# Batch 0's v through casting DMAs, batch 1's loads behind a gate, and a redealt first chain in an attention-and-mixer kernel

## The chip, the cores and the metric

The kernel runs on one core of a Trainium2 chip. The metric is device time in microseconds (us), the median of a few runs. Its engines are TensorE (PE, with its weight loads as PEld), VectorE (DVE), ScalarE (ACT), GpSimd (POOL) and SyncE (SP). DMAs are issued here by SP and by POOL, each into a queue of its own, and run on 16 DMA engines that the core's queues share.

## The reference

Eight batches, eight heads, 576 positions, head size 64. Linear attention gives x for each batch, and a mixer with a low-rank mix over positions and a two-layer product follows:

```
r_q, r_k = relu(q), relu(k)                       # (S, 64) per head
q_p, k_p = [r_q * cos, r_q * sin], [r_k * cos, r_k * sin]      # (S, 128)
kv  = k_p^T v                                     # (128, 64)
z   = sum over S of k_p                           # (128)
x   = (q_p kv) / (q_p z + 1e-6)                   # heads side by side: (576, 512)

u   = x + ((x^T U) V)^T                           # U: 576 x 32, V: 32 x 576
out = u + relu(u w1) w2                           # w1: 512 x 2048, w2: 2048 x 512
```

## The kernel before

The 576 positions of a batch lie in five chunks: four of 128 rows, and a tail (chunk 4) of 64. One partition holds four or five neighbouring positions, so a load of q, k or v is an odd and an even part (`load_odd`, `load_even`, L71 to L81) into the float tiles `qst`, `kst`, `vst`, which all batches share. SP issues them in program order. POOL issues the loads of U and V and of the weights, the latter casting from float to bf16 on the way (`w1_load`, `w2_load`, four loads of 512 KB written each).

The order of work is written out by hand: every engine runs its instructions in program order and waits by semaphores. The stretch that matters here has these steps.

1. Start: memsets, constants, loads of q, k and v of batch 0 on SP, U and V on POOL. POOL's casts of V and U (`cast_uv`). PE runs products of zeros (`keep_warm`, L198).
2. Features of q: `q_prep` (cos and sin weights times relu, L287 on ACT, L289 on DVE), then transposes on PE (`qtr_mm`, L368) and copies to `q_pT` by `qtr_evac`.
3. Features of k, and z by `z_mm` (L883) chunk by chunk, with fillers by `keep_warm` between.
4. `first_chain`: batch 0 from kv to uT. `kv_unit` (L323) makes kv for four heads; `den_mm` (L892) the denominators for four heads; `recip` (L403, L404); `xh_mm` (L903) and `xh_norm` (L912) x for one chunk and four heads; `a_mm` (L439) the product x^T U, called A; `open_mm` (L926) transposes x into a PSUM bank of uT, and `uTd_mm` (L531) adds V's part to it; `uTd_evac` copies uT out. The denominators and z_sb's source lie in the bank pair `xz` (tag X), as does A.
5. The first product with w1 for batch 0, `g1_main` (L551): 16 blocks j of four products each, ACT's relu to `hid` (L560) after each. The first three j begin with half their products, for the first two of four uT parts. Beside the j's run batch 1's steps: `q_prep(1, c)`, `qtr_unit(1, c)` (L356), `k_prep(1, c)`, `v_prep(1, ...)` and batch 0's `u_va` and `u_add` (L464, L473); the table `beside` says after which j each is put.
6. The product with w2 for batch 0 (`g2_part`, L611), with batch 1's kv and x beside it, and so on through the batches.

POOL issues w1's first load between its two casts of batch 0's v tail. Its next steps are the other w1 loads, then a small copy `mark` (L1017) that reads the first half of batch 1's `vst` and so waits for it, then the four w2 loads. SP loads batch 1's q, k and v as soon as the tiles are free, and at slot 15 comes a `gate` (L1033): a tiny DMA that reads a given tile, so that SP stands until this is written, with the loads of batch 2 behind it.

Of the kernel before, what the change touches and what calls it, by code (L numbers as in the profile page):

```python
# [17 lines left out]
def kernel(  # L18
# [91 lines left out]
    def cast(eng, o, i):  # L110
        if eng is nc.scalar:
            nc.scalar.activation(out=o, in_=i, func=AF.Copy, bias=0.0, scale=1.0)
        else:
            eng.tensor_copy(out=o, in_=i)  # L114
# [12 lines left out]
    load_even(qst, q, 0)  # L127
    load_odd(kst, k, 0)
    load_even(kst, k, 0)
    for h0 in (0, 4):  # L130
        load_odd(vst, v, 0, h0, h0 + 4)
        load_even(vst, v, 0, h0, h0 + 4)
    def load_uv():
        nc.gpsimd.dma_start(out=stV, in_=moe_V)
        nines_u = moe_U.rearrange("(m k) r -> m (k r)", k=9)
# [80 lines left out]
    def cast_uv():  # L216
        nine_v = stV.rearrange("r (m k) -> r k m", k=9)
        for i in range(2):
            cast(
                G_,  # L220
                V_nat[:, 0:512].rearrange("r (c m i) -> r c m i", c=4, i=2)[:, :, :, i],
                nine_v[:, 5 * i : 5 * i + 4, :],
            )
        cast(G_, V_nat[:, 512:S], nine_v[:, 4, :])
        cast(G_, U_bf[:, 0:4, :], stU[:, 0:4, :])
        for i in range(2):
            cast(G_, U_bf[tail(i), 4 + i, :], stU[tail(i), 4, :])
# [87 lines left out]
    def kv_unit(b, hg, tag, bufs, eng=None):  # L315
        if b not in kv_sb:
            kv_sb[b] = pool.tile([P, H, E], BF16, tag="kv", bufs=2, name="kv")
        acc = bank([P, 4, E], FP32, tag, bufs, "kv_ps")
        vx = v_ext[b % 2]
        for i in range(4):  # L320
            h = hg * 4 + i
            for c in range(5):
                nc.tensor.matmul(  # L323
                    out=acc[:, i, :],
                    lhsT=k_p[b][:, c, h, :] if c < 4 else k_tl[:, h, :],
                    rhs=v_tl[:, h, :] if c == 4 and b < 2 else vx[:, c, h, :],
                    start=(c == 0),
                    stop=(c == 4),
                )
        cast(eng or V_, kv_sb[b][:, hg * 4 : hg * 4 + 4, :], acc)  # L330

    def kv_pair(b, tag, bufs):
        kv_sb[b] = pool.tile([P, H, E], BF16, tag="kv", bufs=2, name="kv")
# [575 lines left out]
    def xh_norm(b, c, h0, rec, acc):  # L909
        x_alloc(b)  # L910
        rows = slice(0, P) if c < 4 else tail(b)
        nc.vector.tensor_tensor(  # L912
            out=x_of(b, c, rows)[:, h0 * D : h0 * D + 4 * D].rearrange(
                "p (i d) -> p i d", d=D
            ),
            in0=acc[rows],
            in1=rec[rows, c, :].unsqueeze(2).to_broadcast([P if c < 4 else TS, 4, D]),
            op=ALU.mult,
        )

# [3 lines left out]
    def open_mm(b, d, t, cs):  # L924
        for c in cs:
# [2 lines left out]
                start=(c == 0), stop=False,  # L928
            )

    def first_chain(b, xz, v_ps):
        z = xz[:, 0, 0:H]
        d = [
            xz[:, 0, H + 20 * i : H + 20 * i + 20].rearrange("p (c h) -> p c h", h=4)
            for i in range(2)
        ]
        rec = [pool.tile([P, 5, 4], FP32, tag="rec5", bufs=2, name="rec5") for _ in d]
        for h0 in (0, 4):
            v_block(b, h0, h0 + 4, 0, 4, V_)
        cast(V_, V_bf, v_ps.rearrange("r (c p) -> r c p", c=4))  # L940
        cast(A_, z_sb, z)
        kv_unit(b, 0, *T1, A_)
        den_mm(b, 0, 4, d[0])
        recip(rec[0], d[0])
        x0 = [xh_mm(b, c, 0, *t) for c, t in zip(ORD, (G3, G3, G3, OA, OB))]
        den_mm(b, 4, 8, d[1])
        kv_unit(b, 1, *T1, A_)
        for n in range(2):
            xh_norm(b, ORD[n], 0, rec[0], x0[n])
        recip(rec[1], d[1])  # L950
        for n in range(2, 5):
            xh_norm(b, ORD[n], 0, rec[0], x0[n])
        x1 = [xh_mm(b, c, 4, *t) for c, t in zip(ORD[0:4], (G3, G3, G3, OA))]
        for n in range(2):
            xh_norm(b, ORD[n], 4, rec[1], x1[n])
        uT_alloc(b)
        a_ps = xz[:, 1, 0:P]
        a_mm(b, a_ps, (0, 1), range(5))
        cast(A_, A_of(b)[0:TS, :], a_ps[0:TS, :])
        x1.append(xh_mm(b, ORD[4], 4, *G3))  # L960
        for n in range(2, 5):
            xh_norm(b, ORD[n], 4, rec[1], x1[n])
        for i, (tag, bufs) in enumerate((T1, OB, OA)):
            uT_ps[b, i] = bank([P, 4, P], FP32, tag, bufs, "uT_ps")
        for i in range(2):
            open_mm(b, i, uT_ps[b, i], range(4))
        uTd_mm(b, 0)
        uTd_evac(b, 0, A_)
        uTd_mm(b, 1)
        uTd_evac(b, 1, V_)  # L970
        a_mm(b, a_ps, (2, 3), range(5))
        cast(A_, A_of(b)[TS:P, :], a_ps[TS:P, :])
        open_mm(b, 2, uT_ps[b, 2], range(4))
        u3 = ps.tile([P, 2, 512], FP32, tag="X", bufs=1, name="u3")
        uT_ps[b, 3] = u3[:, 0, :].rearrange("p (c t) -> p c t", c=4)
        open_mm(b, 3, uT_ps[b, 3], range(4))
# [40 lines left out]
    G_.tensor_copy(out=mark, in_=vst[0:TS, 3, 4, 0:1])  # L1017
    for n in range(4):
        w2_load(n)
    g1_main(0, 0, True)  # L1020
    uTd_close(0, 2, V_)
    uTd_close(0, 3, A_)
    g1_main(0, 1, True)
    g1_main(0, 2, True)
    q_prep(1, 4, (V_, A_))
    q_prep(1, 0, (V_, V_))


    def at(j, *thunks):
        beside.setdefault(j, []).extend(thunks)  # L1030

    def gate(src):
        nc.sync.dma_start(out=mark2, in_=src)  # L1033
# [12 lines left out]
    for hg in range(2):  # L1046
        at(16 + hg, lambda hg=hg: kv_unit(1, hg, "T", 1))

# [75 lines left out]
```

## Time and profile before

| | |
|---|---|
| median of 3 runs | 301.11 us (299.45 to 301.7) |
| profiled execution, its own time | 301.89 us |
| its span, first to last instruction | 300.1 us |
| mean granted TensorE clock | 0.998 |
| PE busy | 288.3 us (96%) |
| DVE, ACT, POOL busy | 186.3 (62%), 157.4 (52%), 72.7 (24%) |
| DMA | 53.31 MB, mean 178 GB/s |
| chain that ended last | PE 88%, DMA 6%, DVE 2% |
| first product with w1 (L551) | at 23.17 us |
| first product with w2 (L611) | at 40.53 us |

A profile line names the engine, the line of the kernel, the operation, what is written from what, and the count. In a row of the timeline the first two numbers are the start and the length in us; in brackets stands the idle time of the engine before it and what ended it. Matmuls overlap, so a row's length for PE is not the sum of its instructions.

### The profile page before, as it was taken

The page shows a single profiled execution, that of the slowest core. Times are in us where ns is not written, and L with a number is a line of the kernel's source. Part 1 is how long each engine was busy: PE and PEld are TensorE (multiplying, and loading weights), DVE is VectorE, ACT ScalarE, POOL GpSimd, SP SyncE. Part 2 cuts the span into 40 slices and gives each one's busy share as a digit, 9 for nine tenths or more (in the row PEclk, how much of TensorE's full clock was granted, in tenths as well). Part 3 has the DMA queues.
Part 4 walks back from the last instruction along what each step waited for, and adds up shares of the span by engine and source line. Part 5 has one row for each costly group of instructions (what it writes and reads, how often), then busy time and mean ns, then how long its engine had stood idle before and what let it go on. Part 6 is the DMA issues. An engine that isn't in the chain of part 4 may idle for free.

```text
span 300.1 us, 7027 instructions
## 1 busy us (share of the span) xinstructions
PE 288.3 (96%) x2917; PEld 194.5 (65%) x2948; DVE 186.3 (62%) x360; ACT 157.4 (52%) x268; POOL 72.7 (24%) x113
## 2 busy tenths in 40 slices
PE   8999999999989979999999999999999999999993
PEld 6675455545977536865787546865787547845982
DVE  4988748886894657647736577648744685504251
ACT  2935561586672446936584356846693453067300
POOL 8430500050271500550032500550051100400130
PEclk9999999999999999999999999999999999999999
DMA  6999999999979999999659906997366104030004
GB/s 204 351 271 256 219 188 254 284 235 241 278 201 201 131 254 230 210 268 298 177 105 230 336 3 151 223 283 207 72 111 184 39 2 87 2 140 2 0 26 153
DMA packets 85282, 53.31 MB, mean 178 GB/s; under 512 B 54018, under 2 KB 82978, under 8 KB 85250
## 3 DMA queue, kind: packets, MB, share of 16 engines
q1 hardware_dynamic: 78802, 41.40, 59.3%
q0 software_dynamic: 6368, 11.43, 16.2%
q8 instruction: 23, 0.38, 0.5%
q14 instruction: 9, 0.07, 0.1%
q10 hardware_dynamic: 80, 0.03, 0.0%
HBM read 36.86 MB, written 9.44 MB: 154 GB/s over the span
## 4 chain that ended last, share of the span: by engine, by line
PE 88%; DMA 6%; DVE 2%; issue 1%; SPq 1%; ACT 1%; ACTq 0%
PE g_ps L551 35%; PE w_ps L720 27%; PE gt_ps L571 5%; PE o_ps L611 5%; DMA q_pT<-q_p 4%; PE ot_ps L638 3%; PE x_ps L413 3%; DMA qst<-in_q_dram 2%; PE kv_ps L339 2%; PE w_ps L198 1%; PE va_ps L464 1%; PE a_ps L439 1%; PE kv_ps L323 1%; PE t_ps L368 1%; PE t_ps L356 1%
## 5 line engine op out<-in xcount | busy, mean ns | idle before, releaser
L560 ACT ACTIVATE hid<-g_ps 128x512 bf16<-128x512 f32 x128 | 76.1, 597 | 87.2 <-PE g_ps L551 59.9
L551 PE MATMUL g_ps<-uT,w_bf 128*128 128x512 bf16 x491 | 119.4, 379 | 1.3 <-DMA w_bf<-in_moe_w_ch_dram 0.3
L551 PEld LDWEIGHTS <-w_bf 128*128 128x128 bf16 x512 | 46.3, 98 | 49.2 <-issue 0.2
L732 POOL TENSOR_TENSOR o_sb<-w_sum,u_bf 128x512 f32<-128x512 f32 x21 | 26.3, 1278 | 120.7 <-DVE w_sum L732 120.7
L720 PEld LDWEIGHTS <-hid 128*128 128x128 bf16 x448 | 43.7, 98 | 5.6
L720 PEld LDWEIGHTS <-S 128*128 128x128 bf16 x336 | 32.5, 98 | 5.2 <-DVE S L697 1.2
L732 DVE TENSOR_TENSOR o_sb<-o_sb,w_ps 128x512 f32<-128x512 f32 x28 | 19.3, 688 | 18.0 <-PE w_ps L720 11.7
L720 PE MATMUL w_ps<-T,S 128*128 128x256 bf16 x224 | 26.1, 273 | 0.9 <-DVE S L697 0.9
L720 PE MATMUL w_ps<-w_bf,hid 128*128 128x256 bf16 x224 | 26.7, 273 | 0.0
L720 PE MATMUL w_ps<-T,hid 128*128 128x256 bf16 x224 | 26.7, 273 | 0.0
L473 DVE TENSOR_TENSOR u_bf<-x_bf,va_ps 128x1024 bf16<-128x1024 bf16 x16 | 19.3, 1218 | 6.7 <-PE va_ps L464 6.7
L114 POOL CAST v_ext<-vst 128x512 bf16<-128x512 f32 (+1 forms) x30 | 18.6, 658 | 16.8 <-DMA vst<-in_v_dram 13.7
L423 DVE TENSOR_TENSOR x_bf<-x_ps,rec 128x512 bf16<-128x512 f32 x28 | 19.4, 692 | 1.0
L697 DVE TENSOR_TENSOR S<-hid 128x1024 bf16<-128x1024 bf16 x14 | 9.6, 688 | 16.5 <-ACT hid L560 16.5
L403 DVE TENSOR_SCALAR rec<-x_ps 128x8 f32<-128x8 f32 (+1 forms) x35 | 5.8, 164 | 21.7 <-PE x_ps L413 21.6
L287 ACT ACTIVATE k_p<-kst,sinw 128x512 bf16<-128x512 f32 x29 | 18.9, 710 | 0.0
L585 POOL DMA_DIRECT2D out_dram<-o_sb x12 | 7.6, 633 | 44.8 <-DVE o_sb L732 23.2
L413 PEld LDWEIGHTS <-q_pT 128*128 128x128 bf16 x224 | 10.8, 98 | 7.9 <-DMA q_pT<-q_p 2.2
L114 DVE CAST kv<-kv_ps 128x520 bf16<-128x520 f32 (+1 forms) x8 | 5.1, 632 | 17.2 <-PE kv_ps L339 13.7
L287 ACT ACTIVATE q_p<-qst,cosw 128x512 bf16<-128x512 f32 x23 | 15.5, 711 | 0.1
L611 PE MATMUL o_ps<-w_bf,hid 128*128 128x512 bf16 x61 | 15.3, 379 | 0.2
L571 PE MATMUL gt_ps<-uT_tl,w_bf 128*128 128x128 bf16 x256 | 15.1, 219 | 0.0
(145 smaller groups left out, 367.7 us busy)
## 6 DMA issues: line engine op xcount, KB each, us to landing
qst<-in_q_dram SPq DMA_DIRECT2D x14, 512.0 KB, 6.8
kst<-in_k_dram SPq DMA_DIRECT2D x14, 512.0 KB, 8.9
vst<-in_v_dram SPq DMA_DIRECT2D x12, 512.0 KB, 6.8
out_dram<-o_sb POOLq DMA_DIRECT2D x12, 512.0 KB, 6.1
w_bf<-in_moe_w_ch_dram POOLq DMA_DIRECT2D x8, 512.0 KB, 11.1
out_dram<-o_sb SPq DMA_DIRECT2D x4, 512.0 KB, 3.0
qst<-in_q_dram SPq DMA_DIRECT2D x2, 640.0 KB, 7.1
kst<-in_k_dram SPq DMA_DIRECT2D x2, 640.0 KB, 11.0
```

Of the source, the lines that this page charges most:

```text
L114: eng.tensor_copy(out=o, in_=i)
L287: nc.scalar.activation(out=o, in_=i, func=AF.Relu, bias=0.0, scale=w)
L413: nc.tensor.matmul(out=acc[:, g, i * E : i * E + E], lhsT=qT_of(b, c, h), rhs=kv_sb[b][:, h, :], start=True, stop=True,)
L423: nc.vector.tensor_tensor(out=x_of(b, c, rows).rearrange("p (g i d) -> p g i d", g=2, d=D), in0=view[:, :, :, 0:D], in1=rec[rows].unsqueez ...
L473: nc.vector.tensor_tensor(out=u_bf[b][:, d0 : d0 + 2], in0=x_bf[b].rearrange("p c (d n) -> p d c n", n=P)[:, d0 : d0 + 2], in1=va_ps[b, d0 ...
L551: nc.tensor.matmul(out=g_ps.rearrange("p (c t) -> p c t", c=4), lhsT=w1_bf[:, d, j * P : j * P + P], rhs=uT[b][:, d, :, :], start=(d == 0) ...
L560: nc.scalar.activation(out=hid[b][:, j, :], in_=g_ps, func=AF.Relu, bias=0.0, scale=1.0)
L571: nc.tensor.matmul(out=g_ps[:, jj, :], lhsT=w1_bf[:, d, j * P : j * P + P], rhs=uT_tl[pr][:, d, :], start=(d == 0), stop=(d == 3),)
L611: nc.tensor.matmul(out=o, lhsT=hid[0][:, j, cc * P : cc * P + P], rhs=w2_bf[:, j, :], start=(j == 0), stop=(j == NJ - 1),)
L697: V_.tensor_tensor(out=o, in0=a, in1=b_, op=op)
L720: nc.tensor.matmul(out=res[:, g, :], lhsT=lhs[:, k_, g * P : g * P + P], rhs=rhs[:, k_, :], start=(opens and k_ == 0 and g == 0), stop=(k_ ...
L732: eng.tensor_tensor(out=o, in0=x, in1=y, op=ALU.add)
```

## The change

Batch 0's v no longer comes through `vst` and casts. A tile `v0` (it takes the place of the later `hid`) is filled by four casting DMAs that POOL issues, behind its casts of V. The casts of U (`cast_u`) are split off and come after w1's first load. `kv_unit` for batch 0 reads `v0` and makes 64 columns for each head, not 65. `first_chain` makes the denominators of all eight heads at once, with one `recip`, and deals its copies out anew: V's spread copy, both of the first two uT copies and the first x of chunk 3 go to ACT, the second half of A goes to a bank of its own and to DVE, and the last copy of `q_pT` to DVE. Five of the nine fillers beside k's features go. SP has a `gate` on batch 0's kv in front of batch 1's loads. The last two uT products are put ahead of the first w1 products. Batch 1's q features are all given to DVE, after j 2 to 6 (they were ahead of j 0 and after j 0 to 2), its transposes after j 5 to 9 (were 1 to 5), and `spread_tail` after j 12 (was 7).

```diff
@@ start
-    for h0 in (0, 4):
-        load_odd(vst, v, 0, h0, h0 + 4)
-        load_even(vst, v, 0, h0, h0 + 4)
+    v0 = pool.tile([P, H, 5, D], BF16, tag="hid", bufs=1, name="v0")
+    V_.memset(v0[:, :, 4, :], 0.0)
+
+    def v0_load(h0, h1):
+        nc.gpsimd.dma_start(
+            out=v0[1:P:2, h0:h1, 0:4].rearrange("m h c d -> m h (c d)"),
+            in_=nines(v, 0)[:, h0:h1, 5 * D : 9 * D],
+        )
+        nc.gpsimd.dma_start(
+            out=v0[0:P:2, h0:h1].rearrange("m h c d -> m h (c d)"),
+            in_=nines(v, 0)[:, h0:h1, 0 : 5 * D],
+        )
+
@@ kv_unit
-        acc = bank([P, 4, E], FP32, tag, bufs, "kv_ps")
+        n = D if b == 0 else E
+        acc = bank([P, 4, n], FP32, tag, bufs, "kv_ps")
...
-                    rhs=v_tl[:, h, :] if c == 4 and b < 2 else vx[:, c, h, :],
+                    rhs=(
+                        v0[:, h, c, :] if b == 0
+                        else v_tl[:, h, :] if c == 4 and b < 2 else vx[:, c, h, :]
+                    ),
...
-        cast(eng or V_, kv_sb[b][:, hg * 4 : hg * 4 + 4, :], acc)
+        cast(eng or V_, kv_sb[b][:, hg * 4 : hg * 4 + 4, 0:n], acc)
@@ new
+    def xh_norm_act(b, c, h0, rec, acc):
+        x_alloc(b)
+        rows = slice(0, P) if c < 4 else tail(b)
+        for i in range(4):
+            nc.scalar.activation(
+                out=x_of(b, c, rows)[:, (h0 + i) * D : (h0 + i) * D + D],
+                in_=acc[rows, i, :], func=AF.Copy, bias=0.0,
+                scale=rec[rows, c, h0 + i : h0 + i + 1],
+            )
+
@@ first_chain
-        for h0 in (0, 4):
-            v_block(b, h0, h0 + 4, 0, 4, V_)
-        cast(V_, V_bf, v_ps.rearrange("r (c p) -> r c p", c=4))
-        cast(A_, z_sb, z)
+        d = xz[:, 0, H : H + 40].rearrange("p (c h) -> p c h", h=H)
+        rec = pool.tile([P, 5, H], FP32, tag="rec5", bufs=1, name="rec5")
+        cast(A_, z_sb, xz[:, 0, 0:H])
         kv_unit(b, 0, *T1, A_)
-        den_mm(b, 0, 4, d[0])
-        recip(rec[0], d[0])
+        cast(A_, V_bf, v_ps.rearrange("r (c p) -> r c p", c=4))
+        den_mm(b, 0, H, d)
+        recip(rec, d)
         x0 = [xh_mm(b, c, 0, *t) for c, t in zip(ORD, (G3, G3, G3, OA, OB))]
-        den_mm(b, 4, 8, d[1])
         kv_unit(b, 1, *T1, A_)
-        for n in range(2):
-            xh_norm(b, ORD[n], 0, rec[0], x0[n])
-        recip(rec[1], d[1])
-        for n in range(2, 5):
-            xh_norm(b, ORD[n], 0, rec[0], x0[n])
+        xh_norm_act(b, ORD[4], 0, rec, x0[4])
+        for n in range(4):
+            xh_norm(b, ORD[n], 0, rec, x0[n])
...
-        uTd_mm(b, 0)
-        uTd_evac(b, 0, A_)
-        uTd_mm(b, 1)
-        uTd_evac(b, 1, V_)
-        a_mm(b, a_ps, (2, 3), range(5))
-        cast(A_, A_of(b)[TS:P, :], a_ps[TS:P, :])
+        for i in range(2):
+            uTd_mm(b, i)
+            uTd_evac(b, i, A_)
+        a2 = bank([P, P], FP32, *G3, "a_ps")
+        a_mm(b, a2, (2, 3), range(5))
+        cast(V_, A_of(b)[TS:P, :], a2[TS:P, :])
@@ k's features
-    keep_warm(2, *T1)
     for c in TL:
         k_prep(0, c, (V_, A_))
-        keep_warm(2 if c < 2 else 1, *T1)
+        if c < 3:
+            keep_warm((1, 2, 1)[c], *T1)
+        if c == 3:
+            v_ps = spread_v(*OB)
         z_mm(0, c, xz[:, 0, 0:H])
         if c == 1:
             qtr_evac(0, 4, V_, t_q[4])
-    v_ps = spread_v(*OB)
-    qtr_evac(0, 3, A_, t_q[3])
-
-    v_prep(0, 0, 4, (4,), (G_,))
+    qtr_evac(0, 3, V_, t_q[3])
...
+    for h0 in (0, 4):
+        v0_load(h0, h0 + 4)
     w1_load(0)
-    v_prep(0, 4, 8, (4,), (G_,))
+    cast_u()
     for n in range(1, 4):
         w1_load(n)
     first_chain(0, xz, v_ps)
+    gate(kv_sb[0][0:1, 0, 0:1])
     load_odd(qst, q, 1)
...
-    g1_main(0, 0, True)
     uTd_close(0, 2, V_)
     uTd_close(0, 3, A_)
-    g1_main(0, 1, True)
-    g1_main(0, 2, True)
-    q_prep(1, 4, (V_, A_))
-    q_prep(1, 0, (V_, V_))
+    for j in range(3):
+        g1_main(0, j, True)
...
     for n, c in enumerate(ORD):
-        if n > 1:
-            at(n - 2, lambda c=c: q_prep(1, c, (V_, V_)))
+        at(2 + n, lambda c=c: q_prep(1, c, (V_, V_)))
         tg = T1 if n % 2 else O2()
-        at(1 + n, lambda c=c, tg=tg: qtr_unit(1, c, eng=V_, tag=tg[0], bufs=tg[1]))
+        at(5 + n, lambda c=c, tg=tg: qtr_unit(1, c, eng=V_, tag=tg[0], bufs=tg[1]))
...
-    at(7, lambda: spread_tail(*O2()))
+    at(12, lambda: spread_tail(*O2()))
```

More of the change, by code (lines that the diff above doesn't have):

```diff
@@ L224, in cast_uv, with cast_u @@
         cast(G_, V_nat[:, 512:S], nine_v[:, 4, :])
+    def cast_u():
         cast(G_, U_bf[:, 0:4, :], stU[:, 0:4, :])
@@ L916, in xh_norm @@
             in0=acc[rows],
-            in1=rec[rows, c, :].unsqueeze(2).to_broadcast([P if c < 4 else TS, 4, D]),
+            in1=rec[rows, c, h0 : h0 + 4].unsqueeze(2).to_broadcast([P if c < 4 else TS, 4, D]),
             op=ALU.mult,
@@ L929, in open_mm @@
             )
-    def first_chain(b, xz, v_ps):
[L932 to L937, printed above, removed]
-        for h0 in (0, 4):
-            v_block(b, h0, h0 + 4, 0, 4, V_)
-        cast(V_, V_bf, v_ps.rearrange("r (c p) -> r c p", c=4))
-        cast(A_, z_sb, z)
+    def xh_norm_act(b, c, h0, rec, acc):
[7 more added lines that the diff above has]
+            )
+    def first_chain(b, xz, v_ps):
+        d = xz[:, 0, H : H + 40].rearrange("p (c h) -> p c h", h=H)
+        rec = pool.tile([P, 5, H], FP32, tag="rec5", bufs=1, name="rec5")
+        cast(A_, z_sb, xz[:, 0, 0:H])
         kv_unit(b, 0, *T1, A_)
-        den_mm(b, 0, 4, d[0])
-        recip(rec[0], d[0])
+        cast(A_, V_bf, v_ps.rearrange("r (c p) -> r c p", c=4))
+        den_mm(b, 0, H, d)
+        recip(rec, d)
         x0 = [xh_mm(b, c, 0, *t) for c, t in zip(ORD, (G3, G3, G3, OA, OB))]
-        den_mm(b, 4, 8, d[1])
         kv_unit(b, 1, *T1, A_)
-        for n in range(2):
-            xh_norm(b, ORD[n], 0, rec[0], x0[n])
-        recip(rec[1], d[1])
-        for n in range(2, 5):
-            xh_norm(b, ORD[n], 0, rec[0], x0[n])
+        xh_norm_act(b, ORD[4], 0, rec, x0[4])
+        for n in range(4):
+            xh_norm(b, ORD[n], 0, rec, x0[n])
         x1 = [xh_mm(b, c, 4, *t) for c, t in zip(ORD[0:4], (G3, G3, G3, OA))]
         for n in range(2):
-            xh_norm(b, ORD[n], 4, rec[1], x1[n])
+            xh_norm(b, ORD[n], 4, rec, x1[n])
         uT_alloc(b)
@@ L961, in first_chain @@
         for n in range(2, 5):
-            xh_norm(b, ORD[n], 4, rec[1], x1[n])
+            xh_norm(b, ORD[n], 4, rec, x1[n])
         for i, (tag, bufs) in enumerate((T1, OB, OA)):
@@ L993 @@
     xz = ps.tile([P, 2, 512], FP32, tag="X", bufs=1, name="xz")
-    keep_warm(2, *T1)
+    v_ps = None
     for c in TL:
         k_prep(0, c, (V_, A_))
-        keep_warm(2 if c < 2 else 1, *T1)
+        if c < 3:
+            keep_warm((1, 2, 1)[c], *T1)
+        if c == 3:
+            v_ps = spread_v(*OB)
         z_mm(0, c, xz[:, 0, 0:H])
@@ L1000, with gate @@
             qtr_evac(0, 4, V_, t_q[4])
-    v_ps = spread_v(*OB)
-    qtr_evac(0, 3, A_, t_q[3])
-    v_prep(0, 0, 4, (4,), (G_,))
+    qtr_evac(0, 3, V_, t_q[3])
+    def gate(src):
+        nc.sync.dma_start(out=mark2, in_=src)
+    for h0 in (0, 4):
+        v0_load(h0, h0 + 4)
     w1_load(0)
-    v_prep(0, 4, 8, (4,), (G_,))
+    cast_u()
     for n in range(1, 4):
@@ L1019 @@
         w2_load(n)
-    g1_main(0, 0, True)
     uTd_close(0, 2, V_)
     uTd_close(0, 3, A_)
-    g1_main(0, 1, True)
-    g1_main(0, 2, True)
-    q_prep(1, 4, (V_, A_))
-    q_prep(1, 0, (V_, V_))
+    for j in range(3):
+        g1_main(0, j, True)
     def at(j, *thunks):
         beside.setdefault(j, []).extend(thunks)
-    def gate(src):
-        nc.sync.dma_start(out=mark2, in_=src)
     for n, c in enumerate(ORD):
-        if n > 1:
-            at(n - 2, lambda c=c: q_prep(1, c, (V_, V_)))
+        at(2 + n, lambda c=c: q_prep(1, c, (V_, V_)))
         tg = T1 if n % 2 else O2()
-        at(1 + n, lambda c=c, tg=tg: qtr_unit(1, c, eng=V_, tag=tg[0], bufs=tg[1]))
+        at(5 + n, lambda c=c, tg=tg: qtr_unit(1, c, eng=V_, tag=tg[0], bufs=tg[1]))
         at(9 + n, lambda c=c: k_prep(1, c, (V_, A_)))
```

## The prediction

> **What bounds the kernel now.** I read PE's waits first, then the busy time by stretch, then the first 41 us of the timeline, then the DMA queues in that stretch. All times are of the profiled execution, in us from the start of its span. Who made PE wait:
>
> ```profile
> PE x_ps L413 <- DMA q_pT<-q_p: 1.7, 1, 1.7
> PE w_ps L720 <- DVE S L697: 0.9, 1, 0.9
> ...
> PE xh_ps L903 <- ACT kv L112: 0.5, 1, 0.5
> PE u L926 <- ACT A_sb L112: 0.3, 1, 0.3
> PE g_ps L551 <- DMA w_bf<-in_moe_w_ch_dram: 0.3, 1, 0.3
> ```
>
> Once the first product with w1 (L551) has begun, PE waits only twice for longer than 0.3, at 82 (0.9) and at 105.6 (1.7). Busy time by stretch (length, PE, PEld, DVE, ACT, POOL, clock, DMA share, GB/s):
>
> ```profile
> 15.60:23.10 7.50, 6.56 (x160) 5.39 (x161) 5.91 (x17) 2.09 (x6) 2.24 (x3) 1.00 1.16 263
> 23.10:40.50 17.40, 17.23 (x120) 8.70 (x122) 13.76 (x27) 11.54 (x22) 4.45 (x9) 1.00 1.10 223
> 40.50:79.00 38.50, 38.22 (x394) 22.05 (x398) 28.43 (x58) 20.06 (x36) 5.40 (x8) 1.00 1.13 250
> ```
>
> From 23.1 to 79 PE is full, and its work there is not changed. So the change is worth what it moves at 40.5, where PE leaves the first w1 stage for w2 (L611): earlier or later there is earlier or later at the end. The rows of the timeline that I use:
>
> ```profile
> 15.28 0.34 PE L883 MATMUL xz<-v_tl,k_tl 128*128 128x1 bf16 x8
> ...
> 19.06 0.39 ACT L112 ACTIVATE kv<-kv_ps 128x260 bf16<-128x260 f32 x1 [1.98 <-PE kv_ps L323]
> ...
> 23.17 0.38 PE L551 MATMUL g_ps<-uT,w_bf 128*128 128x512 bf16 x1 [0.26 <-DMA w_bf<-in_moe_w_ch_dram]
> ...
> 24.51 0.48 DVE L289 TENSOR_SCALAR q_tl<-qst,cosw 128x512 bf16<-128x512 f32 x1
> ...
> 25.54 0.61 PE L356 MATMUL t_ps<-ident,q_tl 128*128 128x128 bf16 x8
> ...
> 32.19 1.22 DVE L473 TENSOR_TENSOR u_bf<-x_bf,va_ps 128x1024 bf16<-128x1024 bf16 x1 [0.50 <-PE va_ps L464]
> ...
> 33.18 0.18 POOL L1017 COPY mark<-vst 64x1 f32<-64x1 f32 x1 [15.35 <-DMA vst<-in_v_dram]
> ```
>
> The DMA engines are full from 3 to 34. Packets, MB and engine share of the two queues (q0 is POOL's, q1 SP's): first 9 to 16.5 with SP's queue alone, then 20 to 32 with w1 and batch 1 together, then 36 to 46 with the w2 loads nearly alone:
>
> ```profile
> q1 hardware_dynamic: 2386, 2.67, 107.1%
> ```
> ```profile
> q0 software_dynamic: 1420, 1.41, 69.0%
> q1 hardware_dynamic: 1423, 1.59, 46.3%
> ```
> ```profile
> q0 software_dynamic: 1891, 1.89, 116.8%
> ```
>
> SP's queue alone moves 318 packets per us, POOL's nearly alone 189. Together they go packet for packet, 118 per us each. A load of q or k is 1024 packets, a w1 load 512 (2 KB read, 1 KB written each). Landings: w1 at 22.9, 27.4, 31.7 and 36.0; batch 1's q at 18.8, k at 28.6, the last v at 36.3.
>
> **The change part by part.**
>
> v of batch 0. Gone: four loads on SP, two POOL casts (0.41, 0.90), two DVE casts (1.48 together). New: a memset on DVE (0.27, as other 128x256 memsets, while DVE waits for q) and four casting DMAs on POOL behind the V casts that end at 7.83, each 0.67 to 0.91 to issue like L134 and L100. From issue to first packets V took 2.2 (1.81 to 4.0) and the first w1 load 3.2 (13.51 to 16.75), so they start at 10 to 11.1. A casting packet of 1.15 KB has no row: between 318 per us (same bytes read) and 189 (same cast, twice the bytes). I take the first, since full queues in both rows read some 0.37 MB per us. First half landed at 14.0 (bounds 13.4 to 15.6), second at 15.6 (15 to 18.3); k's last packets are held up by 0 to 0.4. They are wanted at 15.1 and 17.4, so I put this at nothing; with that cover gone it is 0.5 to 0.9.
>
> The Trainium skill, SBUF — State Buffer, "SBUF: two separate sides", speaks against this part: descriptors of a DMA issued on POOL can't be written while VectorE runs one of its faster two-port operations. Here w1's first packets come at 16.75, just after DVE's two v casts end at 16.04, while POOL's cast of v took 0.90 beside DVE against 0.41 before; one row fits the rule, none proves it. Its result is a rival below.
>
> POOL behind it: w1's first issue comes at about 11 instead of 13.5, the U casts (1.0) after it; U is wanted at 19.4. w1's packets start when v's end, at 14.4.
>
> First chain. z ends when the last k feature is there (ACT 14.69) plus its eight products: 15.1 instead of 15.62, since five of the nine fillers of PE (L198) go; ACT's copy of q_pT (1.00) becomes one of 0.69 on DVE, beside it. kv products 15.1 to 15.8 (0.71); forty denominators to 16.75 (0.48 per twenty); one add and one reciprocal on DVE of 128x40, between the rows of 128x20 (0.18, 0.28) and twice these, so done at 17.3; ten-product groups as before: second kv 17.45 to 18.1, ACT's copy done at 18.55 (before 19.45). Fresh on ACT: V_bf (0.6, in a hole) and four scalings of 128x64, 0.18 to 0.28 each by L112's small copies, done at 19.3 where A's products want them at 19.4. A copied 20.2, first uT copied by ACT at 21.4, the second behind it at 21.9 (before both by 22.3), A's second half on DVE at 21.5, not on ACT at 22.47. So the last two uT products start at 21.6 instead of 23.17: **1.5 earlier**, bounds 0.8 to 1.8. Putting them before the w1 products costs nothing, all twelve run anyway.
>
> Batch 1's loads. SP now waits in the gate for ACT's first kv copy, 16.25; all eight loads queue behind it, and the first is issued at 17.1 instead of 10.33. For the same pair later (L1033 at 42.53, q issued at 43.40) the packets came at 46, so here at 19.3 to 20.2. By then w1 has had 5 us of the engines alone: 5.2 x 189 = 980 of 2048 packets; the other 1068 need 9 us at 118. q's 1024 need 8.7: last packet at 28.5. Counting packets by half a us, a landing comes 2.3 to 3.3 after the load's last packet under two queues (q 2.3, k 3.0, v's first half 3.3), 1.1 to 1.2 under one (q, k and v of batch 0). w1 is just running out, so I take 2.0: **batch 1's q lands at 30.5**, bounds 28.3 to 31.8, instead of 18.8.
>
> What waits for it. All ten q features are now DVE's, at 2 to 6 of the j order; the transposes of q (L356) at 5 to 9. PE is at the first by 27.3. DVE has had nothing from 22.7 on and stands at the first feature; its in-order work from the landing: ten features at 0.395, two copies at 0.65, one u_add of 1.22, 6.5 in all. The second V product shares bank X with the first (before too) and waits for that u_add. Behind it PE has 28 products of j 9 to 15 (6.05 in the rows 34.5 to 40.5), a transpose group 0.45, V products 0.33, the spread 0.2: 7.1. So PE leaves the stage at landing + 13.6 = **44.1 instead of 40.5: 3.6 later**; the 1.5 of the first chain are lost in the wait (4.2 for the first transposes, 1.0 for bank X). With the landing's bounds: 1.4 to 4.9.
>
> Others queued: k's features and v's casts on DVE then end near 44, before kv wants them; POOL's mark waits for half of v, 34.5 here against 33.2, and the w2 loads behind it land from 41.2, before 44.1. spread_tail at 12: its POOL copies are wanted 20 us later, nothing.
>
> Sum: 301.89 + 3.6 = 305.5 in the terms of the profiled execution, 0.8 above the median of the runs; against that median, 301.11 + 3.6 = **304.7**.
>
> **The rivals.**
>
> A short tail (0.20): q lands with its last packets as under one queue, at 28.3. For it: w1 ends at the same moment. Against: batch 0's v had POOL idle, here it isn't. Then 41.9, 1.4 later: 302.5.
>
> In time (0.13), the other side: batch 1's q lands by 25.5, for instance if SP's queue got its 318 per us while w1 waits. Against: 1420 to 1423 over 12 us. Decides from 26.9 down (26.9 + 13.6 = 40.5). Then the 1.5 would show, but the w2 loads still follow half of v: a landing 6.0 after the mark gives 39.3 to 40.3. So 0.8 earlier: 300.3.
>
> v late (0.10): POOL's casting loads held up by DVE until its run of features ends at 15.3, kv then at 17 and not 15.1, the gate with it, so q 2 later than forecast: 5.6 later, 306.7. For: 16.75 after 16.04. Against: U's packets came at 6.5 with DVE idle, so the lag isn't DVE's alone. This is the time by the skill's rule of the two-port operations.
>
> A slow PE clock (0.07): after 4.2 idle PE runs at half speed for as long as it stood, which puts off 2.1 of work, of which the wait for bank X swallows 1.0: 1.1 more, 305.8. The rows can't decide: the longest wait is 1.7, and the granted clock is 1.00 in every stretch shown. The Trainium skill, TensorE: Matmul & The Clock Gate, "Part 1", says that an idle window of some 3.4 us halves the clock until a busy one has passed; an estimate by its figure is 0.7 more.
>
> **How the numbers follow.** Forecast 0.50, rivals 0.20, 0.13, 0.10, 0.07. One per cent, 3.0, is about what a measurement of this kernel can tell from no change. The forecast is centred 0.6 beyond it with bounds on both sides: 0.32 slower, 0.18 same. Short tail: same 0.20. In time: same 0.09, faster 0.04 (should the waits at 82 or 105 vanish too). v late: slower 0.09, same 0.01. Clock: slower 0.07. Together faster 0.04, same 0.48, slower 0.48. Range 300.3 to 307.2, from the rival in time to v late with half a us; the likeliest alone, 302.5 to 306.0.
>
> **What would show it.** Right: the first w1 product near 21.9; w1's first load landed before 19; q of batch 1 landed near 30.5; PE waiting about 4 for DVE's first q feature near 27 and 1 for u_add; w2's first product near 44. Wrong: q landed before 27; packets of the queues far from one to one; kv products starting after 16; a granted clock below 1.00 near 32; a stage behind 44 that makes up what was lost.

## The result, and the profile after

The changed kernel takes 302.08 us, the median of 20 runs (300.81 to 308.07), against 301.0 of 20 runs of the kernel before. The ratio is 1.0053, with a 95% interval of 1.0031 to 1.0076: some 1.6 us slower, between 0.9 and 2.3. The ratios here and below leave out every execution that took over 1.5% longer than the fastest of the same kernel, while the medians hold all of them. The profiled execution took 302.34, its span is 300.2. Lines of the changed kernel are numbered higher: features L301 (DVE) and L299 (ACT), batch 1's transposes L372, w1 products L567, w2 products L627, kv L336, z L899, `mark` L1041, the gate L1024.

PE's waits (us in total, times, longest):

```profile
PE t_ps L372 <- DVE q_tl L301: 1.8, 1, 1.8
PE x_ps L429 <- DMA q_pT<-q_p: 1.4, 2, 1.1
...
PE xz L899 <- DVE k_p L301: 1.0, 2, 0.5
PE va_ps L480 <- DVE u_bf L489: 0.5, 1, 0.5
```

Two waits are new in the first w1 stage: 1.8 for DVE's first feature of batch 1's q, and 0.5 for `u_add`. A third, 1.0 in two parts, stands where the fillers were. The busy time by stretch shows the same hole: PE works 15.11 of the 17.4 us from 23.1, before 17.23.

```profile
15.60:23.10 7.50, 6.98 (x172) 5.70 (x170) 4.70 (x14) 3.99 (x12) 0.00 (x0) 1.00 1.23 213
23.10:40.50 17.40, 15.11 (x112) 7.90 (x111) 11.99 (x25) 9.15 (x17) 3.15 (x5) 1.00 0.94 248
40.50:79.00 38.50, 38.48 (x375) 21.07 (x373) 28.01 (x58) 20.29 (x37) 5.77 (x11) 1.00 1.15 235
```

The rows of the timeline that answer to those shown of before:

```profile
15.48 0.34 PE L899 MATMUL xz<-v_tl,k_tl 128*128 128x1 bf16 x8
...
16.47 0.39 ACT L112 ACTIVATE kv<-kv_ps 128x256 bf16<-128x256 f32 x1 [0.43 <-PE kv_ps L336]
...
22.59 1.69 PE L567 MATMUL g_ps<-uT,w_bf 128*128 128x512 bf16 x7
...
28.79 0.48 DVE L301 TENSOR_SCALAR q_tl<-qst,cosw 128x512 bf16<-128x512 f32 x1 [5.41 <-DMA qst<-in_q_dram]
...
29.73 0.62 PE L372 MATMUL t_ps<-ident,q_tl 128*128 128x128 bf16 x8 [1.79 <-DVE q_tl L301]
...
33.95 1.22 DVE L489 TENSOR_TENSOR u_bf<-x_bf,va_ps 128x1024 bf16<-128x1024 bf16 x1
...
42.28 1.03 PE L627 MATMUL o_ps<-w_bf,hid 128*128 128x512 bf16 x4
```

The second kv copy of the first chain ends at 19.05 (18.66 and 0.39; before at 19.45), the first w1 product starts 0.6 earlier, and the first product with w2 comes at 42.28: 1.75 later than the 40.53 of before. DVE stands idle for 5.41 before that q feature, with the load of q as its releaser.

The two queues of the DMA engines, in the stretches 13.2 to 21.9, 21.9 to 24.4 and 24.4 to 26.9 (packets, MB, engine share):

```profile
q0 software_dynamic: 1793, 1.75, 123.1%
q1 hardware_dynamic: 16, 0.01, 0.6%
```
```profile
q0 software_dynamic: 304, 0.31, 71.9%
q1 hardware_dynamic: 302, 0.31, 44.3%
```
```profile
q1 hardware_dynamic: 711, 0.82, 92.2%
q0 software_dynamic: 83, 0.07, 17.3%
```

w1 has the engines to itself for 8.7 us and moves 206 packets per us. Batch 1's q, issued at 17.75 and 18.50, has its first packets only at about 21.8. It shares the engines from 21.9 on for 2.5 us, packet for packet, then has them almost alone, and its last packet passes at 26.9.

Downstream the offset shrinks: batch 2's kv products come 1.76 later than before (72.05 against 70.29), batch 4's 0.9 (131.16 against 130.25). The waits at 82 and 105, 0.9 and 1.7 before, are 0.2 here and, in two parts, 1.4. This pair of executions differs by 0.45 at the end, while the runs differ by 1.6: what comes back behind 79 varies between executions (the same wait of PE for `q_pT` is 3.0 in one experiment and 0.2 in others). So the experiments are read at the first product with w2, which is at 40.53 before, and in the times. "Landing + 13.5" below means that this product starts 13.5 us after DVE's (or ACT's) first feature of batch 1's q.

### The profile page after: what moved, and what is told of

Same layout as the page of the kernel before. It is cut to its first block, busy times and chain, and to the rows that moved or that the text cites. A ratio compares the mean times of both kernels' runs of the same rounds, so it can differ in the third digit from the quotient of the medians.

```text
span 300.2 us, 7040 instructions
## 1 busy us (share of the span) xinstructions
PE 289.3 (96%) x2943; PEld 193.4 (64%) x2943; DVE 185.0 (62%) x357; ACT 157.4 (52%) x271; POOL 73.2 (24%) x115
## 4 chain that ended last, share of the span: by engine, by line
PE 85%; DMA 8%; DVE 5%; issue 0%; DVEq 0%
PE g_ps L567 33%; PE w_ps L736 28%; DMA qst<-in_q_dram 5%; PE gt_ps L587 5%; PE o_ps L627 5%; PE ot_ps L654 4%; DMA q_pT<-q_p 3%; PE x_ps L429 3%; PE kv_ps L355 2%; DVE q_p L301 1%; PE va_ps L480 1%; PE a_ps L455 1%; PE kv_ps L336 1%; PE t_ps L372 1%; DVE k_p L301 0%
## 5 line engine op out<-in xcount | busy, mean ns | idle before, releaser
L567 PE MATMUL g_ps<-uT,w_bf 128*128 128x512 bf16 x512 | 120.2, 379 | 0.0
L567 PEld LDWEIGHTS <-w_bf 128*128 128x128 bf16 x512 | 46.4, 98 | 49.8 <-issue 0.2
L748 POOL TENSOR_TENSOR o_sb<-w_sum,u_bf 128x512 f32<-128x512 f32 x21 | 26.3, 1274 | 120.1 <-DVE w_sum L748 120.1
L489 DVE TENSOR_TENSOR u_bf<-x_bf,va_ps 128x1024 bf16<-128x1024 bf16 x16 | 19.3, 1215 | 5.1 <-PE va_ps L480 5.1
L419 DVE TENSOR_SCALAR rec<-x_ps 128x8 f32<-128x8 f32 (+1 forms) x35 | 5.8, 164 | 21.7 <-PE x_ps L429 21.6
L299 ACT ACTIVATE k_p<-kst,sinw 128x512 bf16<-128x512 f32 x29 | 18.9, 711 | 0.3 <-DMA kst<-in_k_dram 0.3
L627 PE MATMUL o_ps<-w_bf,hid 128*128 128x512 bf16 x64 | 15.6, 379 | 0.0
L299 ACT ACTIVATE q_p<-qst,cosw 128x512 bf16<-128x512 f32 x23 | 15.5, 711 | 0.1
L587 PE MATMUL gt_ps<-uT_tl,w_bf 128*128 128x128 bf16 x256 | 15.1, 219 | 0.0
```

Source lines behind the costliest of these rows:

```text
L299: nc.scalar.activation(out=o, in_=i, func=AF.Relu, bias=0.0, scale=w)
L489: nc.vector.tensor_tensor(out=u_bf[b][:, d0 : d0 + 2], in0=x_bf[b].rearrange("p c (d n) -> p d c n", n=P)[:, d0 : d0 + 2], in1=va_ps[b, d0 ...
L567: nc.tensor.matmul(out=g_ps.rearrange("p (c t) -> p c t", c=4), lhsT=w1_bf[:, d, j * P : j * P + P], rhs=uT[b][:, d, :, :], start=(d == 0) ...
L587: nc.tensor.matmul(out=g_ps[:, jj, :], lhsT=w1_bf[:, d, j * P : j * P + P], rhs=uT_tl[pr][:, d, :], start=(d == 0), stop=(d == 3),)
L627: nc.tensor.matmul(out=o, lhsT=hid[0][:, j, cc * P : cc * P + P], rhs=w2_bf[:, j, :], start=(j == 0), stop=(j == NJ - 1),)
L748: eng.tensor_tensor(out=o, in0=x, in1=y, op=ALU.add)
```

## The experiments

My theory was that the gate costs the time because it delays q's landing, and that the stream of v and w1 packets ahead of q sets the landing, not the distance from the gate. The rivals: the missing fillers (a slower PE clock), ten features on one engine, a first chain or a v that isn't earlier at all. Each ratio is to the kernel before, with its 95% interval.

**e1, the gate left out.**

```diff
-    gate(kv_sb[0][0:1, 0, 0:1])
```

> The changed kernel without the gate in front of batch 1's loads. Theory A (the loss sits in the gate: batch 1's q lands at 28.8 us in the changed kernel, and PE leaves the first w1 stage 13.5 us after that landing): q is issued at about 11 us, its first packets come near 14, shared packet for packet with w1 it lands near 25; the first w1 product stays near 22.6; no wait of PE for the first q transposes; the first w2 product near 39.6, limited by the w2 loads behind half of v; total about 0.9 us below the kernel before, 2.5 below the changed one. Rival B (what is lost is lost in the first chain and its engines, the gate is only beside it): the first w2 product stays near 42, total stays 1.6 above before. Rival C (without the gate batch 0's v comes late): kv products after 17 us, w1's first load after 22.6, total not below the kernel before.

300.82 us, ratio 0.9989 (0.9951 to 1.0027); against the changed kernel that is 0.994, with both intervals taken together 0.989 to 0.998. The loss is gone, and no gain takes its place. PE doesn't wait for batch 1 any more. Yet in the profiled execution (305.83, 5.0 above the median) the clock had halved from 15.0 to 25.2. The first w1 product came at 25.40, and the first w2 product at 42.56, where 39.6 was expected, with PE busy all the way from 23.1. So this profile doesn't show what the gate does at 40.5; e6 shows it. The busy time of the stretch that holds the first chain:

```profile
15.60:23.10 7.50, 7.03 (x135) 6.27 (x132) 3.85 (x11) 2.35 (x8) 0.00 (x0) 0.50 1.16 252
```

PE is as full there as in the changed kernel, but gets through 135 products instead of 172.

**e2, q's features split between DVE and ACT, the gate kept.**

```diff
-        at(2 + n, lambda c=c: q_prep(1, c, (V_, V_)))
+        at(2 + n, lambda c=c: q_prep(1, c, (V_, A_)))
```

> The changed kernel with batch 1's q features shared by DVE (cos) and ACT (sin) instead of all ten on DVE. Theory A (behind the late landing of q it is DVE's chain of ten features, two copies and one u_add, 6.5 us, that sets the stage's end): five features of 0.395 us less on DVE, q lands at 28.8 as before, the wait for bank X goes, the first w2 product near 41.3 instead of 42.3, total about 1.0 us below the changed kernel. Rival B (PE's own work behind the landing sets the end): the first w2 product within 0.3 us of 42.3 and the total unchanged. Rival D (ACT's relu, queued behind the features that wait for q, holds PE back): the first w2 product later than 42.3.

301.97 us, ratio 1.0031 (0.9987 to 1.0074). Inconclusive: the profiled execution had the halved clock from about 16.3 to 26.5, its first w1 product at 25.59, q at 29.35 and the first w2 product at 43.21, where 41.3 was expected. e10 repeats it without the halved clock.

**e3, the gate on v instead of kv.**

```diff
-    gate(kv_sb[0][0:1, 0, 0:1])
+    gate(v0[0:1, 4, 0, 0:1])
```

> The changed kernel with the gate on the landing of batch 0's v (15.05 us) instead of batch 0's first kv (16.86 us), so batch 1's loads are issued about 1.8 us earlier. Theory S (q's landing is set by the stream of everything ahead of it, w1 too: the two queues run out at about the same time): q's first packets come near 20 instead of 21.9 but share with w1 for longer, so q lands at 28.8 again within 0.5 us, and the first w2 product stays near 42.3. Rival I (the landing follows the issue at a fixed distance, 10.3 us in the changed kernel): q lands at 27.0, the first w2 product near 40.5, total 1.8 us below the changed kernel.

302.58 us, ratio 1.0067 (1.0025 to 1.0109). SP issued the gate at 14.97 and not 16.88, and q at 15.85 and not 17.75, 1.9 earlier. The timeline's rows of the first feature and the first w2 product:

```profile
28.97 0.49 DVE L301 TENSOR_SCALAR q_tl<-qst,cosw 128x512 bf16<-128x512 f32 x1 [3.68 <-DMA qst<-in_q_dram]
...
42.47 1.03 PE L627 MATMUL o_ps<-w_bf,hid 128*128 128x512 bf16 x4
```

q lands no earlier. A fixed distance from issue to landing would have given 27.0, so the packets ahead of it set the landing. In the stretch from 15.6 the clock was 0.55 in this execution, the first w1 product came at 24.50, 1.9 later than in the changed kernel, and still the w2 product stands at landing + 13.5, as there. Behind a late q, these 7 us of slow clock at the start cost nothing. The 10 us of e2 were too long for that: there PE was busy for all of the 17.4 us from 23.1 and waited for nothing, and the w2 product came 0.9 later than in the changed kernel.

**e4, the first chain alone**: the kernel before with the redealt `first_chain` and with the last two uT products ahead of w1's; v, fillers, loads and batch 1's steps as before.

```diff
...
+        d = xz[:, 0, H : H + 40].rearrange("p (c h) -> p c h", h=H)
+        rec = pool.tile([P, 5, H], FP32, tag="rec5", bufs=1, name="rec5")
...
+            uTd_evac(b, i, A_)
...
+    for j in range(3):
+        g1_main(0, j, True)
```

> The kernel before with the redealt first chain alone: one row of denominators, ACT and DVE copies as in the changed kernel, the last two uT products ahead of the first w1 products. v comes by SP's loads and DVE casts, there is no gate, and features, transposes and fillers stand as before. Theory A (the chain itself is shorter, but w1's first load lands at 22.9 there, so little of it shows): the last two uT products near 22.4 instead of 23.5, the first w1 product at 22.9 to 23.1, the first w2 product 0.5 to 0.7 us earlier than before, total 0.6 below. Rival B (the redealt chain is longer, since ACT now carries copies that DVE carried): the first w1 product after 23.2, total above the kernel before.

300.81 us, ratio 0.999 (0.995 to 1.0031). The last uT products stand at 22.75 and the first w2 product at 40.24, 0.3 earlier than before, where 0.5 to 0.7 was expected. By itself this part is worth that at 40.5, and nothing that the times show.

**e5, the changed kernel with all nine fillers.**

```diff
+    keep_warm(2, *T1)
...
-        if c < 3:
-            keep_warm((1, 2, 1)[c], *T1)
+        keep_warm(2 if c < 2 else 1, *T1)
```

> The changed kernel with PE's fillers of the kernel before (2 ahead of k's features, then 2, 2, 1, 1, 1). In the runs so far the mean granted clock of the changed kernel and its relatives was mostly 0.983 to 0.994, in two profiles 0.50 from 15 or 16 us to 25 or 26, where the kernel before and the chain alone, which have these fillers, show 0.994 to 1.000. Theory F (without five fillers PE stands idle enough ahead of 15 us for its clock to be halved): mean clock 0.996 to 1.000 in nearly all runs, no stretch at 0.50, the first w1 product near 22.6 us every time; q still lands at 28.8 and the first w2 product stays near 42.3, so the total stays 0.5 to 1.5 us above before. Rival V (the slower DVE features beside POOL's casting loads leave PE idle, the fillers don't matter): clock 0.985 to 0.99 again.

303.0 us, ratio 1.0062 (1.0017 to 1.0107): no better than the changed kernel, though its mean clock was 0.992 or less in only 2 of 12 executions, against 13 of 20. The wait stays:

```profile
PE x_ps L429 <- DMA q_pT<-q_p: 3.0, 1, 3.0
...
PE t_ps L372 <- DVE q_tl L301: 1.2, 1, 1.2
PE va_ps L480 <- DVE u_bf L489: 0.5, 1, 0.5
```

q at 28.63, the w2 product at 42.13: again landing + 13.5. So the fillers are not the cause of the loss.

**e6, all fillers and no gate** (the edits of e5 and e1 together).

> The changed kernel without the gate and with the fillers of the kernel before. If gate (late q) and fillers (halved clock) are the two causes of the loss and there is no third, the first w1 product comes near 22.6 us, q's landing stops nobody, the first w2 product comes at 39.5 to 40.0 and the total is 0.7 to 1.2 us below the kernel before. Rival (the engines that redealt copies went to, or w1 beside batch 1's loads, lose it again): the first w2 product after 40.5, total not below before.

299.96 us, ratio 1.0000 (0.997 to 1.003). Taking the gate from e5 takes 0.6% off (0.994, with both intervals taken together 0.988 to 0.999). The expected gain of 0.7 to 1.2 us below the kernel before didn't come. The rival's numbers did, but not by its causes: another wait takes the gain of the early chain.

```profile
PE o_ps L627 <- DMA w_bf<-in_moe_w_ch_dram: 0.7, 1, 0.7
```

Its rows of the timeline:

```profile
25.94 0.49 DVE L301 TENSOR_SCALAR q_tl<-qst,cosw 128x512 bf16<-128x512 f32 x1 [2.03 <-DMA qst<-in_q_dram]
...
35.18 0.18 POOL L1040 COPY mark<-vst 64x1 f32<-64x1 f32 x1 [21.08 <-DMA vst<-in_v_dram]
...
41.10 1.04 PE L627 MATMUL o_ps<-w_bf,hid 128*128 128x512 bf16 x4 [0.66 <-DMA w_bf<-in_moe_w_ch_dram]
```

PE doesn't wait for batch 1's q, although it comes at 25.94. POOL holds the w2 loads until half of batch 1's v is there, at 35.18 and not 33.18 as before, and w2 arrives 0.66 after PE wants it.

**e7, v alone**: the kernel before with `v0`'s four casting loads, w1 and the casts of U behind them.

```diff
...
-    v_prep(0, 0, 4, (4,), (G_,))
+    for h0 in (0, 4):
+        v0_load(h0, h0 + 4)
     w1_load(0)
-    v_prep(0, 4, 8, (4,), (G_,))
+    cast_u()
```

> The kernel before with batch 0's v by the four casting DMAs and w1 and the U casts behind them, all else as before: old chain, old fillers, no gate. Theory A (v's part costs the chain nothing but slows DVE's features to 0.6 us each while POOL issues, 7.8 to 10.3): clock 0.996 or more, kv products near 15.8, w1's first load lands at 18 to 20 instead of 22.9, the first w2 product 0 to 0.4 us earlier than before, total within 0.5 us of before. Rival (v late): kv products after 16.5, total above before.

299.82 us, ratio 1.0007 (0.9974 to 1.004). No change: the first w1 product stands at 22.94 (23.17 before), `mark` at 34.51, the w2 product at 40.90, 0.4 later than before where 0 to 0.4 earlier was expected. Batch 1's q comes at 25.06 here, 6.2 later than before, behind the one stream of v and w1, and PE waits 0.2 for it.

**e8, the gate alone**: the kernel before, with SP standing for batch 0's first kv copy ahead of batch 1's loads.

```diff
+    nc.sync.dma_start(out=mark2, in_=kv_sb[0][0:1, 0, 0:1])
```

> The kernel before with the gate on batch 0's first kv in front of batch 1's loads, all else as before. By theory A and the stream: w1 starts at 16.8 us as before and runs alone until q's packets come near 21.5; w1's last 1100 packets and q's 1024 then take 8.6 us, q lands at 32. The transposes stand after j 1 to 5 there, so PE waits from about 24.5 to 32.8, and the first w2 product comes at 47.5 to 48.5, 7 to 8 us later than before; 1 to 2 more if the long wait halves PE's clock; total 308.5 to 311. Rival (the landing follows the issue at 10.3): q lands at 28.2, 4 us later at the w2 product, total 305.5.

308.99 us, ratio 1.0286 (1.023 to 1.0341). q landed at 31.49, where 32 was expected, and with batch 1's steps where the kernel before has them PE meets the full delay:

```profile
PE t_ps L356 <- ACT q_tl L287: 6.7, 1, 6.7
```

Batch 1's kv products come at 51.09, 9.5 later than before: 6.7 of wait and the halved clock behind it, both expected. The stretch from 23.1:

```profile
23.10:40.50 17.40, 10.72 (x67) 6.13 (x66) 7.02 (x14) 4.51 (x8) 3.09 (x5) 0.71 1.01 266
```

Here the clock goes to 0.50 within PE's one long wait and stays there until past 37. That agrees with the Trainium skill, TensorE: Matmul & The Clock Gate, "Part 1", by which the clock is halved after an idle window of some 3.4 us. In the changed kernel the wait is 1.8, and the clock behind it stays at 1.00.

**e9, e6 with one w2 load ahead of `mark`.**

```diff
+    w2_load(0)
...
-    for n in range(4):
+    for n in range(1, 4):
```

> The version with fillers and without the gate, and in it the first w2 load issued ahead of the small copy that waits for half of batch 1's v (the other three behind it as before). In that version without this edit q landed at 25.9 us, PE waited for nothing of batch 1, but POOL's copy came at 35.2 and PE waited 0.7 us for w2's first load, the first w2 product came at 41.1. Theory W (the gain of the early q went into this wait): no wait for w2, the first w2 product at 40.2 to 40.5, as in the kernel with the chain alone, total 0.6 to 0.9 us below that version, 0.3 to 0.9 below before. Rival (the w2 load takes packets from batch 1's v, which then holds the kv products of batch 1): PE waits near 42 to 44 for v, total not below.

300.11 us, ratio 0.9972 (0.9935 to 1.0008). The wait for w2 is gone:

```profile
40.21 1.03 PE L627 MATMUL o_ps<-w_bf,hid 128*128 128x512 bf16 x4
```

This is 0.9 earlier than in e6, while `mark` moves to 37.15. It has the lowest ratio of all, but isn't shown to beat the kernel before. Against the changed kernel it is 0.9972 / 1.0053 = 0.992, with both intervals taken together 0.988 to 0.996.

**e10, e5 with q's features split** (the edits of e5 and e2 together).

> The changed kernel (gate as it is) with the fillers of the kernel before and the q features shared by DVE and ACT. The same split without the fillers ran under a halved clock and told nothing. Theory A (behind the landing of q DVE's chain sets the end): q lands at 28.6 to 28.8, no wait for u_add, the first w2 product at 41.0 to 41.4 instead of 42.1, total 0.7 to 1.1 us below the version with fillers alone. Rival B (PE's own work sets it): first w2 product within 0.3 of 42.1. Rival D (ACT's relu behind the features holds PE): later than 42.1.

301.82 us, ratio 1.0047 (1.0008 to 1.0086). The profile shows what the split moves:

```profile
PE t_ps L372 <- ACT q_tl L299: 1.3, 1, 1.3
```

q at 28.82, the wait for `u_add` gone, the w2 product at 41.66: 0.5 earlier than e5, that is landing + 12.8. So the dealing to DVE alone is worth 0.5 to 0.7 of the loss at 40.5, and the rest is the landing. The times don't resolve it: the ratios of e5 and e10 differ by 0.0015, less than their intervals.

**e11, e4 with the changed kernel's few fillers.**

```diff
-    keep_warm(2, *T1)
...
-        keep_warm(2 if c < 2 else 1, *T1)
+        if c < 3:
+            keep_warm((1, 2, 1)[c], *T1)
```

> The kernel with the chain alone (v by SP's loads, no gate, mean clock 0.994 to 1.000) with the changed kernel's four fillers instead of nine. Theory F (missing fillers alone halve the clock): clock 0.985 to 0.994 in most runs, a stretch at 0.50 from about 15 us in the profile, the first w1 product after 24 there, total 0.5 to 2 us above the chain alone. Theory F+V (it takes the slower DVE features of the casting loads as well): clock 0.996 or more in most runs, the first w1 product at or before 23.1.

300.54 us, ratio 0.9994 (0.9959 to 1.0029). Of 10 executions six had a clock of 0.977 to 0.992; e4's twelve all had 0.994 to 1.0. So the missing fillers alone bring the lower clock. The profiled execution had 1.00, so no trace of e11 shows the stretch, and the expected 0.5 to 2 us above e4 is not to be seen in the ratio. In that profile kv's first product came at 15.17, the last uT products at 21.79 and the first w2 product at 40.00.

**e12, e9 with the fillers moved** to the places of PE's gaps (the fillers' part of the edit, against the changed kernel).

```diff
+    keep_warm(2, *T1)
...
-            keep_warm((1, 2, 1)[c], *T1)
+            keep_warm(2, *T1)
```

> As the version with the first w2 load ahead, but with the fillers where PE waits anyway: two ahead of k's features and two behind each of the first three, none behind the last two (eight in all). Theory: these eight lie within PE's waits for DVE's features, so the clock stays at 0.996 or more and the kv products start at 15.7 instead of 16.2, the first w1 product near 22.6, the first w2 product near 39.8, total 0.8 to 1.4 us below the kernel before. Rival (the last two fillers are needed): clock 0.985 to 0.99, total as before or above.

302.26 us, ratio 0.9999 (0.9956 to 1.0043). The first w1 product comes at 22.33, the earliest of all, but four of twelve executions had a clock of 0.983 to 0.989, and the next waits are there: 0.4 for w1, and behind the first w2 product, at 40.11, 1.0 in four parts for batch 1's v. No gain.

## Why the prediction was right and wrong

**Right: the sign, the mechanism, the chain behind the landing.** q's landing behind the gate sets 40.5. Landing + 13.6 was forecast; the profile has 42.28 - 28.79 = 13.5, e3 and e5 also 13.5. The waits were named rightly too: for DVE's first q feature, and for `u_add`. e6 against e5 shows the gate to be the cause, and e8 shows it alone.

**Wrong: the landing, 30.5 forecast, 28.79 measured.** That is 1.7 of the 1.85 by which the forecast of 3.6 later was too much at 40.5 (1.75 measured). The step that failed is the one that counted w1's progress before q, 980 of 2048 packets with 1068 left to share; q met 387 in the run. Three of its terms were off:

- v's casting packets started at about 10.2, 2.4 after their first issue, and were through at about 13.2 and not 14.4. In the 3.2 us from 10.0 the queue moved 1019 packets, so my rate of 318 per us was right or a little low; the start was near the early bound of 10 to 11.1.
- w1 alone moved 206 per us, not 189. My 189 was the rate of the w2 loads.
- q's first packets came at about 21.8 and not at 19.3 to 20.2. That let w1 go on alone, so that q met 387 packets of the other queue instead of 1068.

The third does not matter for the landing here: the engines were never idle, w1 ran out before q, and in e3 q's packets came at about 19.7 and it landed no earlier. The whole stream gives it: 13.2 + 2048 / 206 = 23.1 for w1, and 1024 / 318 = 3.2 more for q is 26.3, against 26.9 measured. POOL's queue in fact moved 2180 packets from 13.2 to 26.9, 132 more than w1's loads have; what these are is open, but with them the sum is 27.0. With the terms of the prediction the same sum is 14.4 + 10.8 + 3.2 = 28.4, its last packet of q. The tail behind the last packet, 2.0 forecast, was 1.9. So the rival "a short tail" was near in size, 41.9 for 42.28, by luck: the tail was long, the stream was early.

**The first chain: 1.5 forecast, 0.6 to 0.9 measured.** The last uT products start at 22.27. The prediction set them against 23.17, but that row before is the first w1 product, and the uT products came behind it:

```profile
23.48 0.39 PE L531 MATMUL uT_ps<-V_bf,A_sb 32*128 32x512 bf16 x1
```

PE does this work in the other order now, so 23.17 is still the start to compare with, and the gain is 0.9 by it and 0.6 by the first w1 products. z ended at 15.82, before at 15.62, and not at 15.1: DVE's features of q were slower (last section) and k's with them, 12.42 for 11.76. The gain was lost in the wait for q, as I had said.

**Price of v at nothing**: right for its landing, wrong for its issue. It landed at 12.5 and 15.05, and PE's kv products waited for z's k features, not for v. The rival "v late" fell with that: the casting loads were not held up by DVE. But while POOL issued them, DVE's features were slower, which the prediction had nowhere in its sum. From DVE's first feature to kv's first product it took 8.14 us here and 7.80 in e1, but 7.48 in e11, which has the few fillers and no casting loads. There the last uT products came at 21.79, near the forecast 21.6. So v cost the first chain some 0.3 to 0.7.

**In time**, the other side, is what e6 shows, with q at 25.94 (the point was 26.9). The limit that this rival named is there too, w2 behind half of v, but later: 41.10, where the rival had said 39.3 to 40.3.

**The clock**: behind the wait for q it did not fall. It fell elsewhere, at 15 to 16 in the profiles of e1, e2 and e3, where the changed kernel took the fillers away, a step that I had priced by its gain alone. In the changed kernel this seems to hide behind q: its 13 executions with a mean clock of 0.992 or less have a median of 301.74, the other seven 302.34.

**From 40.5 to the end** I carried the whole shift over. The profile pair gave back 0.9 of it at the waits of 82 and 105, which I had quoted and not used; over the runs some 1.6 of 1.75 are left.

## What to carry to other kernels

Where a load that is held back meets a queue that runs out before it, as q met w1 here, it lands when all of these packets are through, whichever queue they are in: add up the stream, each kind at its own measured rate, and don't trust the distance from issue to landing. Where the other queue is longer, as without the gate, count packet for packet: q in e6 landed at 25.94 while w1's packets still ran at some 120 per us beside batch 1's. Before moving a load earlier or later, look for the transfer due next behind it, here the w2 loads behind half of v, since it takes over the gain. Work that looks idle, such as products of zeros, may be holding up the clock. A load's issue can cost another engine time, even where its data come early enough.

## What the runs showed of the hardware that was not expected

**The clock halves without a long idle stretch.** In e3 and in the changed kernel PE's rows are the same to 0.1 us from 5 to 15.5, and to 0.01 us from 10.6 on, with no gap above 0.6; from 11.5 to 15.5 it is busy 3.04 of 4.00 us. In e3's profiled execution the clock then drops; its busy time us by us, with the clock behind the five engines:

```profile
14.00:15.00 1.00, 0.59 (x11) 0.34 (x9) 1.00 (x4) 0.91 (x2) 0.04 (x1) 1.00 1.23 203
15.00:16.00 1.00, 1.00 (x25) 0.77 (x25) 0.92 (x2) 0.14 (x1) 0.00 (x0) 0.77 1.25 207
16.00:17.00 1.00, 1.00 (x28) 1.00 (x26) 0.00 (x0) 0.09 (x2) 0.00 (x0) 0.50 1.26 209
```

It stays at 0.50 for some 7 us, 10 in e1 and e2. In the changed kernel's profiled execution it does not drop, but the mean clock of 13 of its 20 runs is 0.992 or less. The kernel before, with 3.89 busy of the same 4.00, has 0.996 or more in most of its runs beside the experiments. What decides between executions of one program is open. So is the price where nothing hides it: the ratios of e11 and e4, or e1 and e6, differ by less than their intervals. But within one kernel the executions sort by the clock: in e1 the three with 0.993 or more took 299.76 to 300.19 and the other nine, with 0.989 or less, 300.41 to 305.83; in e11 the four with 0.994 or more took 299.08 to 300.45 and the other six 300.33 to 305.34. This doesn't prove that the clock is the cause.

**While POOL issues casting DMAs, DVE is slower.** While POOL issued v's four loads (7.78 to 10.25), DVE's first four q features took 2.39 us, before 1.68 (the row of before first):

```profile
8.18 1.68 DVE L289 TENSOR_SCALAR q_p<-qst,cosw 128x512 bf16<-128x512 f32 x4 [3.71 <-DMA qst<-in_q_dram]
```
```profile
7.55 2.39 DVE L301 TENSOR_SCALAR q_p<-qst,cosw 128x512 bf16<-128x512 f32 x4 [2.83 <-DMA qst<-in_q_dram]
```

It is so in every profile: all six features of q take 3.0 to 3.7 us in the kernels with these loads and 2.4 to 2.6 in the four without. The Trainium skill, SBUF — State Buffer, "SBUF: two separate sides", has a two-port operation of VectorE lock GpSimd out, so that it can't write the descriptors of such DMAs, and whichever of the two starts first blocks the other. Here v's first packets came some 2.4 after the issue with DVE busy, V's 2.2 with DVE idle. So no hold-up of the packets is seen, and the loss is DVE's; that the ports are its cause is not shown.

**A load of SP's queue behind a full POOL queue** took 4.0 us from its issue to its first packet (17.75 to 21.8), where v's on POOL took 2.4. In e3, issued 1.9 earlier, it landed no earlier. The full queue alone doesn't explain the 4.0: before, a load of SP's issued at 43.40 beside w2's packets had its first packets at 46.
